# Ranking rows of a top-k gate: a row sent through DRAM, and compares cut into three parts

## The chip, the cores and the metric

The kernel runs on one core of a Trainium2 chip. The metric is the device time of one execution in microseconds (us); less is better. A core has five engines with queues of their own: TensorE (PE; its weight loads are shown as PEld), VectorE (DVE), ScalarE (ACT), GpSimd (POOL), and SyncE (SP), which here only issues DMAs. Each engine works through its instructions in the order in which they were written, and waits on semaphores for the others.

## The reference

Attention with a choice of key chunks, and then a mixture of experts in which each expert keeps at most 80 tokens. Cut to what matters here:

```python
# attention: 4 batches, 8 heads, 768 positions, head size 64  ->  x of 3072 rows of 512
logits = x @ w_gate                       # 8 experts
expert_idx = np.argmax(logits, axis=1)
probs = np.exp(logits - logits.max(-1, keepdims=True))
probs /= probs.sum(-1, keepdims=True) + 1e-09
gate_w = probs[np.arange(N), expert_idx]
for e in range(E):
    tok_idx = np.where(expert_idx == e)[0]
    if len(tok_idx) > capacity:                       # 80
        keep = np.argpartition(-gate_w[tok_idx], capacity)[:capacity]
        tok_idx = tok_idx[keep]
    h = np.maximum(x[tok_idx] @ w1[e], 0.0)
    out[tok_idx] = gate_w[tok_idx, None] * (h @ w2[e])
```

To keep the 80 strongest tokens of an expert, the kernel counts for each token how many tokens of the same expert have a larger gate value (or an equal one and an earlier place). That count is the token's rank. It is made batch by batch, 768 tokens at a time, and the batches' tables are merged.

## The kernel before, in words

The main loop has 16 rounds, `i` from 0 to 15, each for one pair of heads (4 pairs per batch). A round makes scores on TensorE (lines L512 and L527), exponentials on ScalarE (L534), masked copies and sums of exponentials on GpSimd (L548 is a select, L557 an add into `ES`), row sums on TensorE (L584 and L598) with their transpose on VectorE (L589), the transposed rows of the pair before (L644 on TensorE, scaled by L664 on VectorE and stored to DRAM by L666 through SP), the values (L571), and the preparations of later pairs: `take_q` (L442), `bounds` (L475), `bounds_out` (L482 to L494), `take_k` (L452 to L459), `unselT` (L500). The order of all instructions is written out by hand, and each engine keeps it. Loads of q, k and v are issued by SP two to four rounds ahead; one expert weight of 2 MB per round is issued by GpSimd (`wload`, L412 and L415).

A helper (`op`) keeps for each named resource who wrote and read it last, and puts in the semaphore waits. A name that two instructions write makes the second wait for the first, on the same engine too, except on TensorE.

The gate work of batch `bb` is woven into the four rounds of the next batch, `i = 4 * (bb + 1) + kk`; the last batch's comes after the loop and has functions of its own. For the first three batches:

- `kk = 0` (rounds 4, 8, 12): `gate_in`, `gate_exp`, `gate` make the gate value `gt6` (128 partitions by 6 tiles) and the chosen expert `ohb`. Near the end of the round `rank_own` (L729) multiplies each token's value with a triangle of factors that settles ties, into the scratch `T1`. Then `rank_row` spreads the 768 values of the batch along the free dimension of all partitions: six transposes on TensorE (L719) into the score bank `SC[1]`, and one copy to `G` on ScalarE (L721).
- `kk = 1` (rounds 5, 9, 13): `rank_pred` (L724) makes a copy of the row that is smaller by one part in 2^24; `rank_cmp` of tile 5 (L744) follows on VectorE, ahead of the row scaling L664. At the end of the round come `rank_diag` (L737, two instructions) and `rank_cmp` of tiles 4, 3, 2, 1, 0 (L744). Each `rank_cmp` compares 640 columns of the row, in a rotated order: from the tile behind the diagonal onwards and around, in which the smaller copy stands ahead of the true one so that one compare serves both sides of the diagonal.
- `kk = 2` (rounds 6, 10, 14): `rank_count` (L794) sums the compares per expert with 44 matmuls on TensorE, ahead of L644 of that round. `rank_slot` and, later, `rank_late` turn the counts into slots. In `kk = 3` `table` (L817) and `merge` follow.

The compares are kept in bf16 in places that hold weights only later. `Cs` gives the place, and `Ck` the resource name, which is that of the whole weight tile:

```python
def Cs(b, jt, n, lo, w):
    t, o = (w1s[E - 1], jt * S) if jt < NT - 1 else (w2s[E - 2], 2 * S)
    return bass.AP(t, o + lo, [[DB * Fd, 128], [S, n], [1, w]])
def Ck(b, jt):
    return [f"w1_{E - 1}" if jt < NT - 1 else f"w2_{E - 2}"]
```

The last batch has no rotation: `last_diag` (L756, one instruction per tile), `last_low` (L764, or two of ScalarE, L766 and L767) and `last_high` (L771) compare the columns of the diagonal, below and above it, and `last_count` (L778) uses 24 matmuls of 192 columns. Its order on the engines stands after the loop.

## Time and profile before

| | |
|---|---|
| median of 3 runs | 291.2 us (290.19 to 293.35) |
| the profiled execution | 290.18 us |
| its span, from first to last instruction | 288.4 us |
| mean granted TensorE clock | 0.997 |
| PE busy | 273.8 us (95%) |
| DVE busy | 210.4 us (73%) |
| ACT busy | 146.9 us (51%) |
| POOL busy | 227.2 us (79%) |
| DMA | 47.95 MB in 158359 packets |

Busy time counts the engine's own instructions; waiting and the issue of DMAs are not counted. In a timeline a row is: start, length, engine, line, operation, output and inputs, shapes, and how many instructions of the kind follow each other ("x5"). Behind a row, in brackets, stands idle time of the engine before it and who ended it. In a view of one line the three numbers are the shortest, the median and the longest in ns.

### The profile page before, as it was taken

What the parts mean: (1) busy time and instruction counts of PE and PEld (TensorE: products, weight loads), DVE (VectorE), ACT (ScalarE), POOL (GpSimd) and SP (SyncE); (2) the same over time, 40 slices, a digit from 0 to 9 for tenths busy, and PEclk for the clock granted to TensorE, in tenths of its full rate; (3) what the DMA queues carried; (4) which work ended last, traced back from release to release, by engine and by line L of the source; (5) the groups of instructions that cost most, each with busy time, mean ns of one, the idle gap of its engine ahead of it and who ended that gap; (6) DMA issues with size and microseconds to landing.
All of it is one profiled execution on the core that took longest, in us unless ns stands there. A gap on an engine that the chain in (4) does not pass through costs nothing.

```text
span 288.4 us, 8693 instructions
## 1 busy us (share of the span) xinstructions
PE 273.8 (95%) x3606; PEld 169.4 (59%) x3609; DVE 210.4 (73%) x575; ACT 146.9 (51%) x202; POOL 227.2 (79%) x296
## 2 busy tenths in 40 slices
PE   7995999999999999999999999999999999979991
PEld 7553465656565556656655656766565666537761
DVE  5885282739697989676979897899799888933341
ACT  2281645565657555656575556565756672603310
POOL 5059899999899999998999999989999992034532
PEclk9999999999999999999999999999999999999998
DMA  9999969989999999999999989996997959921211
GB/s 151 179 152 144 309 113 294 200 127 181 182 178 155 204 167 202 164 179 164 178 164 184 193 152 160 165 173 126 270 220 143 303 81 189 193 56 50 85 60 60
DMA packets 158359, 47.95 MB, mean 166 GB/s; under 512 B 142405, under 2 KB 150721, under 8 KB 158320
## 3 DMA queue, kind: packets, MB, share of 16 engines
q1 hardware_dynamic: 141664, 28.34, 50.0%
q0 software_dynamic: 13520, 18.67, 38.2%
q10 hardware_dynamic: 3136, 0.39, 0.9%
q8 instruction: 28, 0.46, 0.7%
q14 instruction: 11, 0.09, 0.1%
HBM read 53.49 MB, written 11.01 MB: 224 GB/s over the span
## 4 chain that ended last, share of the span: by engine, by line
PE 66%; POOL 18%; DVE 7%; DMA 4%; issue 2%; ACT 1%; ACTq 1%; POOLq 0%; DVEq 0%
PE SC L512 20%; PE OB L571 19%; POOL ES L557 12%; PE SC L527 4%; PE OB L1139 4%; PE M L598 3%; POOL EXB L548 3%; PE OB L644 3%; PE SC L1115 3%; PE M L475 3%; PE M L584 2%; PE MB L500 2%; DMA x_rows<-xp 1%; DMA qn<-in_q_dram 1%; DMA qn<-x_rows,idx 1%
## 5 line engine op out<-in xcount | busy, mean ns | idle before, releaser
L534 ACT ACTIVATE EXB<-SC 128x1024 f32<-128x1024 f32 x96 | 86.2, 917 | 46.4 <-PE SC L527 45.1
L557 POOL TENSOR_TENSOR ES<-ES,EXB 128x256 f32<-128x256 f32 (+1 forms) x105 | 101.8, 982 | 4.8
L512 PE MATMUL SC<-qT,kT 64*128 64x512 f32 (+3 forms) x512 | 96.3, 466 | 0.1
L571 PE MATMUL OB<-EXB,vn 128*64 128x256 f32 (+3 forms) x704 | 73.0, 361 | 2.9 <-POOL EXB L548 2.8
L571 PEld LDWEIGHTS OB<-EXB,vn 128*64 128x64 f32 x704 | 46.8, 137 | 26.4 <-issue 9.1
L512 PEld LDWEIGHTS SC<-qT,kT 64*128 64x128 f32 x512 | 41.4, 186 | 23.0 <-issue 14.3
L557 POOL TENSOR_TENSOR ES<-EXB 128x768 f32<-128x768 f32 (+1 forms) x30 | 46.9, 1562 | 2.5
L527 PE MATMUL SC<-unsT,ind 64*128 64x128 bf16 (+5 forms) x256 | 37.7, 289 | 0.1
L579 ACT ACTIVATE oT<-OB 128x512 f32<-128x512 f32 (+1 forms) x32 | 15.6, 489 | 42.1 <-PE OB L571 42.1
L548 POOL TENSOR_SCALAR_AFFINE_SELECT EXB<-EXB 128x256 f32<-128x256 f32 x79 | 34.1, 443 | 0.0
L589 DVE STREAM_TRANSPOSE M<-M 128x192 f32<-128x192 f32 x16 | 6.3, 394 | 23.6 <-PE M L598 23.0
L527 PEld LDWEIGHTS SC<-unsT,ind 64*128 64x128 bf16 x256 | 12.8, 95 | 17.9 <-issue 8.0
L442 DVE STREAM_TRANSPOSE qT<-qn 128x768 f32<-128x768 f32 x16 | 15.6, 975 | 7.4 <-PE SC L527 6.6
L664 DVE TENSOR_TENSOR xp<-OB,rden 128x768 bf16<-128x768 f32 x16 | 15.3, 954 | 6.6 <-PE OB L644 6.2
L446 ACT ACTIVATE rq<-qT 128x768 f32<-128x768 f32 x16 | 13.5, 843 | 8.5 <-DVE qT L442 7.9
L1092 POOL DMA_INDIRECT qn<-x_rows,idx x4 | 3.9, 987 | 17.5 <-DVE kT L1155 16.5
L452 DVE STREAM_TRANSPOSE kT<-kn 128x768 f32<-128x768 f32 x16 | 15.5, 967 | 1.3 <-DMA kn<-in_k_dram 1.3
L1145 POOL DMA_INDIRECT out_dram<-EXB,idR x6 | 5.9, 991 | 12.3 <-DVE EXB L1143 8.9
L456 DVE TENSOR_REDUCE kmm<-kT 128x24 f32<-128x768 f32 x16 | 15.2, 950 | 0.5
L457 DVE TENSOR_REDUCE kmx<-kT 128x24 f32<-128x768 f32 x16 | 15.1, 942 | 0.0
L489 DVE MAX8 top<-M 128x8 f32<-128x8 f32 (+4 forms) x160 | 14.6, 164 | 0.6
L644 PE MATMUL OB<-ident_f,oT 128*128 128x128 f32 x96 | 13.9, 281 | 0.5 <-ACT oT L579 0.5
(223 smaller groups left out, 411.5 us busy)
## 6 DMA issues: line engine op xcount, KB each, us to landing
w1s<-in_moe_w_dram POOLq DMA_DIRECT2D x8, 1024.0 KB, 9.9
w2s<-in_moe_w_dram POOLq DMA_DIRECT2D x7, 1024.0 KB, 10.7
vn<-in_v_dram SPq DMA_DIRECT2D x32, 192.0 KB, 4.5
kn<-in_k_dram SPq DMA_DIRECT2D x62, 96.0 KB, 2.7
qn<-in_q_dram SPq DMA_DIRECT2D x62, 96.0 KB, 3.1
out_dram<-w1s SPq DMA_DIRECT2D x3, 1536.0 KB, 9.1
x_rows<-xp SPq DMA_DIRECT2D x16, 192.0 KB, 5.2
out_dram<-G SPq DMA_DIRECT2D x1, 1536.0 KB, 8.2
```

Source lines behind the costliest of these rows:

```text
L442: op("dve", lambda: ve.transpose(qT[j][:], qn[s][:].rearrange("p a b c -> p (a b c)")), r=[f"qn{s}{g}" for g in range(4)], w=[f"qT{j}"])
L452: op("dve", lambda: ve.transpose(kT[j][:], kn[s][:].rearrange("p a b c -> p (a b c)")), r=[f"kn{s}{g}" for g in range(4)], w=[f"kT{j}"])
L456: op("dve", lambda: ve.tensor_reduce(kmm[j][:, 0, 0:NCH], kv, AX, ALU.min), r=[f"kT{j}"], w=[f"kmm{j}"])
L512: op("pe", lambda: pe.matmul(o, kT[j][pr, ts(kt)], qT[j][pr, q0:q1], start=True, stop=False), r=[f"kT{j}", f"qT{j}"], w=[f"SC{s}"], inc=False)
L527: op("pe", lambda: pe.matmul(o, ind[pr, ts(kt)], unsT[j][pr, b0 - 128:q1 - 128], start=False, stop=True), r=[f"ind{h}", f"unsT{j}"], w=[f" ...
L534: op("act", lambda: ac.activation(Ex(st, None, 0, W), src, ACTF.Exp, scale=SCALE), r=[f"SC{s}"], w=[f"E{st}"])
L548: op("gp", lambda: gp.affine_select(ad, a, pattern=[[0, 2], [1, 128]], compare_op=ALU.is_ge, fill=0.0, base=0, channel_multiplier=-1), r=[ ...
L557: op("gp", lambda: gp.tensor_tensor(o, in0, in1, ALU.add), r=[f"E{s2}", f"E{first[0]}"] if first else [f"E{s2}"] + kt, w=kt)
L571: op("pe", lambda: pe.matmul(OB[pr, q0:q1], vn[s][:, kt, h, :], ex, start=(n == 0), stop=last), r=[f"vn{s}{h}", "ES0" if st is None else f ...
L579: op("act", lambda: ac.activation(oT[:, q0:q1], OB[:, q0:q1], ACTF.Copy), r=[f"O{bk}"], w=[f"oT{bk}"])
L644: op("pe", lambda: pe.transpose(OB[:, ts(t)], oT[:, ts(t)], ident_f[:]), r=["oT0", "oT1", "ident_f"], w=[f"O{t // 4}"], inc=(t in (3, NT - ...
L664: op("dve", lambda: ve.tensor_tensor(xo, xi, rx, ALU.mult), r=["O0", "O1", "rden"], w=[f"xp{i % 2}"])
```

## The change

For the first three batches the gate row no longer goes through TensorE. VectorE transposes `gt6` (now 32 columns wide) in blocks of 32, SP writes the result to a DRAM tensor `gate_row` in the order of the tokens, and reads it back to all 128 partitions. `row_out` stands behind `gate` in rounds 4, 8, 12, that is behind the row store L666 on SP's queue; `row_in` stands ahead of the q and k loads of that round. Both DMAs wait in SP's queue, the second for the landing of the first.

`rank_pred` and `rank_own` are gone. The compares of all batches are those of the last batch: `diag`, `low`, `high`, in unrotated places. In the first three batches `low` of tile 5 stands where `rank_cmp` of tile 5 stood, and all others follow at the end of rounds 5, 9, 13. `count` has 24 matmuls for every batch. The resource names of the scratch places remain (`Cw`). The last batch keeps its order and its engines.

```diff
-                gt6 = al(pers, "gt6", [128, NT])
+                gt6 = al(pers, "gt6", [128, 32])
+                gtT = al(pers, "gtT", [128, 32])
...
-                def rank_row(b):
-                    for t in range(NT):
-                        gb = bass.AP(gt6, t, [[NT, 128], [0, 128]])
-                        op("pe", lambda: pe.transpose(SC[1][:, ts(t)], gb, ident_f[:]),
-                           r=["gt6", "ident_f"], w=["SC1"], inc=(t == NT - 1))
-                    op("act", lambda: ac.activation(G[:, S:2 * S], SC[1][:, 0:S], ACTF.Copy), r=["SC1"], w=["grow"])
...
+                def row_out():
+                    op("dve", lambda: ve.transpose(gtT[:], gt6[:]), r=["gt6"], w=["gtT"])
+                    o = bass.AP(gd.tensor, gd.offset, [[32, 4], [128, 32], [1, 32]])
+                    op("sp", lambda: sp.dma_start(o, gtT[:]), r=["gtT"], w=["gd"], dsem="d_gd")
+
+                def row_in():
+                    a = bass.AP(gd.tensor, gd.offset, [[0, 128], [1, S]])
+                    op("sp", lambda: sp.dma_start(G[:, S:2 * S], a), r=["gd"], w=["grow", "growA", "growB"], dsem="d_gr")
...
+                def Cw(b, jt):
+                    return Ck(b, jt) if b < B - 1 else []
...
-                def last_diag(*jts):
+                def diag(b, *jts):
                     for jt in jts:
-                        op("dve", lambda: ve.scalar_tensor_tensor(Cl(jt, jt * 128, 128), triQ[:], gt6[:, jt:jt + 1],
+                        op("dve", lambda: ve.scalar_tensor_tensor(Cl(b, jt, jt * 128, 128), triQ[:], gt6[:, jt:jt + 1],
                                                                   G[:, S + jt * 128:S + (jt + 1) * 128], ALU.mult, ALU.is_ge),
-                           r=["triQ", "gt6"] + gk(jt * 128, jt * 128 + 128), w=[f"D{jt}"])
+                           r=["triQ", "gt6"] + gk(jt * 128, jt * 128 + 128), w=[f"D{jt}"] + Cw(b, jt))
...
-                               r=["ohb", f"D{jt}"] + ([f"L{jt}"] if jt else []) + ([f"U{jt}"] if jt < NT - 1 else []),
+                               r=["ohb", f"D{jt}"] + ([f"L{jt}"] if jt else []) + ([f"U{jt}"] if jt < NT - 1 else []) + Cw(b, jt),
...
                     if live and kk == 1:
-                        rank_pred()
-                        rank_cmp(bb, 5)
+                        low(bb, 5)
...
                     if live and kk == 2:
-                        rank_count(bb)
+                        count(bb, (5, 0, 4, 1, 3, 2))
                         rank_slot(bb)
...
                         gate(bb)
+                        row_out()
...
+                    if live and kk == 0:
+                        row_in()
                     if i + 4 < NP:
                         load(i + 4, "qk")
...
-                    if live and kk == 0:
-                        rank_own(bb)
                     if live and kk == 1:
-                        rank_diag(bb)
-                        rank_cmp(bb, 4, 3, 2, 1, 0)
+                        diag(bb, *range(NT))
+                        for jt in (0, 4, 1, 3, 2):
+                            if jt:
+                                low(bb, jt)
+                            high(bb, jt)
...
-                    if live and kk == 0:
-                        rank_row(bb)
```

`low` and `high` get their scratch names in the same way as `diag`.

## The prediction

> **What bounds the kernel now.** I read the page first, for the engine that works longest and for the chain that ended last, and then the windows of four successive rounds of the loop over head pairs (a round runs from one end of L598 to the next). Times without another label are microseconds on the clock of the profile of before; "round i" is the loop index.

> ```profile
> PE 273.8 (95%) x3606; PEld 169.4 (59%) x3609; DVE 210.4 (73%) x575; ACT 146.9 (51%) x202; POOL 227.2 (79%) x296
> ...
> PE 66%; POOL 18%; DVE 7%; DMA 4%; issue 2%; ACT 1%; ACTq 1%; POOLq 0%; DVEq 0%
> ```

> TensorE sets the end, and POOL takes it over for a sixth of the chain.

> ```profile
> 59.99:73.91 13.92, 13.92 (x167) 8.36 (x165) 9.47 (x26) 7.89 (x10) 12.83 (x17) 1.00 1.02 166
> 73.91:88.49 14.58, 14.58 (x172) 8.95 (x171) 12.60 (x32) 8.70 (x13) 13.67 (x17) 1.00 1.01 174
> 88.49:104.36 15.87, 15.81 (x177) 9.22 (x179) 14.68 (x31) 8.95 (x12) 15.11 (x20) 1.00 1.18 180
> 104.36:117.23 12.87, 12.87 (x201) 7.90 (x197) 11.12 (x34) 7.54 (x10) 12.47 (x15) 1.00 1.04 187
> ```

> The columns are length, then busy time of PE, PEld, DVE, ACT and POOL. A round without gate work (3) takes 13.92 and PE fills it; POOL is 12.8 busy, so it has about one microsecond to spare. Rounds 4, 5, 6 carry gate row, compares and count of batch 0. Round 4 is longer by the 0.66 of the six transposes L719. In round 5 VectorE has 14.7 of work: its queue is where the change falls. The timeline of VectorE there, and then of POOL:

> ```profile
> 99.03 0.81 DVE L737 TENSOR_TENSOR w2s<-w2s,G 128x128 bf16<-128x128 f32 x1
> 99.87 1.30 DVE L737 TENSOR_TENSOR w1s<-w2s,G 128x640 bf16<-128x640 f32 x1
> 101.21 3.30 DVE L744 TENSOR_SCALAR w1s<-G,gt 128x640 bf16<-128x640 f32 x5
> 104.43 0.38 DVE L589 STREAM_TRANSPOSE M<-M 128x192 f32<-128x192 f32 x1
> ```

> ```profile
> 100.57 1.19 POOL L557 TENSOR_TENSOR ES<-ES,EXB 128x256 f32<-128x256 f32 x1
> 101.72 0.49 POOL L459 TENSOR_TENSOR kmm<-kmx,kmm 128x24 f32<-128x24 f32 x1
> ...
> 103.01 0.54 POOL L548 TENSOR_SCALAR_AFFINE_SELECT ES<-EXB 128x256 f32<-128x256 f32 x1
> 103.51 0.65 POOL L548 TENSOR_SCALAR_AFFINE_SELECT EXB<-EXB 128x256 f32<-128x256 f32 x1
> 104.25 1.94 POOL L557 TENSOR_TENSOR ES<-EXB 128x768 f32<-128x768 f32 x1
> ```

> The two engines take turns. The compare of 128 columns takes 0.81, though 128 elements need little: it ends 0.15 after POOL's add (98.42 to 99.69). POOL's next add but one takes 1.19 instead of its usual 0.73, since it starts only when the compare of 640 columns ends at 101.17. The same from the view of one line:

> ```profile
> L744 DVE TENSOR_SCALAR w1s<-G,gt x15: 553/570/904, 101.2 to 219.8; 128x640 bf16<-128x640 f32 x15
> L744 DVE TENSOR_SCALAR w2s<-G,gt x3: 2041/2044/2054, 89.6 to 205.5; 128x640 bf16<-128x640 f32 x3
> ```

> The same compare takes 0.55 when POOL leaves it alone and 2.04 when it starts just behind POOL's 1.81 add. So each compare issued during an add waits that add out, and POOL then goes first again before the next compare. Last, TensorE at the place where the compares are used:

> ```profile
> 104.76 0.28 PE L527 MATMUL SC<-unsT,ind 64*128 64x256 bf16 x2
> 104.96 0.28 PE L794 MATMUL MB<-w2s,ohb 128*32 128x32 bf16 x8
> 105.07 0.60 PE L794 MATMUL MB<-w1s,ohb 128*32 128x64 bf16 x36
> 105.60 0.88 PE L644 MATMUL OB<-ident_f,oT 128*128 128x128 f32 x6
> ```

> The count L794 starts as soon as the scores end. The last compare ended at 104.51, 0.4 before: there is almost no slack between VectorE's compares and TensorE.

> **The change, part by part.** *Gate row.* Six transposes (L719) and their copy (L721, 0.81 on ACT) go. They are on TensorE's path: -0.66 per batch. L724 (0.83, ACT) goes too and is worth nothing, for ACT is 51% busy. L729 (1.40, VectorE, end of round 4) goes, worth nothing: VectorE idles 1.26 after it. Added is one transpose of 128x32 on VectorE; by L589 (0.40 for 192 columns) and the smallest rows (0.16) it costs 0.2, hidden because VectorE's bound scores are ready about 0.8 before TensorE asks for them in round 4.

> *Two DMAs on SP.* In round 4 SP is behind: it issues the row store L666 at 83.94, though its data were ready at 78.07. So the write of the gate row issues near 84.5, and SP, which now waits for its landing, issues the read that much later. The row store of that round landed 3.45 after its issue; so the read goes out near 87.9, and POOL's weight load, issued at 87.34 or 0.7 earlier, runs against it. The nearest rows for the read bound it by 2.0 (an idle-queue load of kn) and 10.0 (kn issued at 88.07). I take 3.5, because it has 128 pieces of 3 KB where a load has 768 of 128 bytes, but shares with the weights: landed near 91.4. Its first reader, the compare of tile 5, would then wait about 2.4 on VectorE; the row scaling L664 behind it ends 1.0 late and so does everything on VectorE up to the chain of compares. In rounds 8 and 12 SP is not behind that far (L666 at 136.65 and 194.15) and the read lands before its reader. Queued behind the wait on SP are the q, k and v loads; they have two rounds to land and keep some 7 of slack, so nothing there.

> *Compares.* Seven instructions in the end of round 5 (two L737, five L744) become fifteen: six diagonal ones of 128 columns, and nine low or high parts of 128 to 640. From the last batch's rows, a diagonal is 0.346 and a part 0.281 (128 columns) to 0.554 (640), that is about 0.21 fixed and the rest by columns. The scratch tile is one resource in the bookkeeping, so each compare waits for the one before and they follow 0.04 apart. Undisturbed this is 6 x 0.39 + 9 x 0.25 + 1.67 = 6.2, to 105.3. Now the turns with POOL, in order from 99.03. D0, D1, D2 each wait out one of the adds that end at 99.69, 100.49, 101.29: done 101.42. D3 to D5 run while POOL issues its weight load: 102.57. High 0 shares with the first select, 103.24; low 4, 103.78. POOL's 768-column add takes the port until 105.46: high 4, 105.53. Low 1 beside a select: 105.89. The 1.27 add: high 1, 107.44. Low 3 beside a select: 107.92. The 1.28 add: high 3, 109.21. Then POOL has no more exponentials to add, and low 2 and high 2 end at 110.04. The same bookkeeping gives 104.49 for the chain of before, where the trace has 104.51. Bounds: 105.3 (no turns) to 110.5 (if the chain starts 1.0 late, as in batch 0).

> *Count.* 24 matmuls replace 44 over as many columns, so 0.64 stays. From the second tile on, each waits for the last compare, because all name the same scratch tile: 20 of the 24 come after 110.08 and take 0.53. Behind them on TensorE stand L644 and the last scores. L644 starts at 110.6 instead of 105.60: +5.0 per batch. VectorE's L589 also waits, but its scaled rows are due only at 113.0, before the values want them (113.7).

> [...]

> *Clock.* TensorE would idle from 105.0 to 110.1, 5.1 long. The trace shows an idle gap of 2.77 (22.6 to 25.38) after which the matmuls ran as before, and the end, where the last matmul ends at 282.59 and the clock reads half from 286.9, 4.3 later:

> ```profile
> 282.60:286.80 4.20, 0.00 (x0) 0.00 (x0) 0.48 (x1) 0.00 (x0) 0.97 (x1) 1.00 0.21 81
> 286.90:288.40 1.50, 0.00 (x0) 0.00 (x0) 0.00 (x0) 0.00 (x0) 0.00 (x0) 0.50 0.00 0
> ```

> At the start L884's matmuls came 0.107 apart from 1.75 to 7.0 and 0.056 after: 5.25 at half speed cost 2.6. So per gap 0 to 2.6. 5.1 lies nearer to the gap that fell, but with 0.8 to spare on one sample; I take half, 1.3 per batch. [...]

> *Sum.* 3 x (-0.66 + 5.0) = 13.0; batch 0's late row 0.4; clock 3.9: +17.3. The profiled execution took 290.18 (span 288.4, 1.8 around it); the median of the runs shown is 291.2. 290.18 + 17.3 = 307.5, and half a microsecond towards the median: 308.

> **The rivals.** *The row lands behind the weights.* If the read is held like kn at 88.07, it lands near 98, the compare of tile 5 and L664 wait, and TensorE loses 6 more in batch 0: 314; in all three batches 326. For it: three of four kn loads there took 9.4 or more. Against: its pieces are few, and in batches 1 and 2 it is issued earlier.
> *The turns cost little.* Then the chain ends at 105.3, L644 starts at 105.9, +0.3 - 0.66 per batch: 289.1, or 290 at the median. Against: every compare of round 5 that met an add waited for it.
> *Faster.* The compares end before TensorE asks (104.9), so the transposes' 0.66 is won and also the 0.27 by which POOL's held-up adds delay L598 in round 5: 3 x 0.93 = -2.8, 287.4 to 288.2. What decides is the chain's end: the three waits for long adds would have to vanish and the fixed cost to fall by a few hundredths each. I see nothing for that but the shorter work per instruction.

> **How the numbers follow.** Forecast 0.78, row behind weights 0.09, little cost 0.07, faster 0.06. From the forecast's bounds: without any loss of clock 303.6, with all of it 311.5; one add less in each chain takes 3.8 off (300), a late row adds 6 to a case without clock loss or 2 to the top. So 300.5 to 314. About 1% is what a measurement can tell here; faster by more 0.05, within 0.08, slower 0.87.

> **What would show it.** Right: fifteen compares in rounds 5, 9, 13, several over 1.2; L589 of rounds 6, 10, 14 about 5.5 later in its round; a gap of some 5 in PE ahead of the second tile of the count; no L719. Wrong: compares of 0.3 to 0.6 throughout, or a gap of PE ahead of L571 in round 5 (the row). A clock below 1 after the gaps tells how much of the term was due.

## The result, and the profile after

The changed kernel takes 311.06 us (309.89 to 311.52, 4 runs) against 291.5 (290.19 to 293.35, 4 runs) before: 1.066 times, interval 1.059 to 1.073. The profiled execution took 311.52, its span 309.6 against 288.4. Of some kernels below the executions differ by several per cent from one to the next; their ratio leaves out those more than 1.5% above the fastest, so the whole spread stands beside it.

The page of the changed kernel: the engines, the granted clock in 40 slices, the chain that ended last, and the count's group, whose last column is TensorE's idle time ahead of it.

```profile
PE 279.8 (90%) x3528; PEld 173.2 (56%) x3531; DVE 215.8 (70%) x600; ACT 142.4 (46%) x196; POOL 221.8 (72%) x296
...
PEclk9997999999999979999999689999998699999997
...
PE 64%; DVE 23%; DMA 5%; issue 3%; POOL 3%; ACTq 1%; POOLq 0%; DVEq 0%
...
L760 PE MATMUL MB<-w1s,ohb 128*32 128x192 bf16 x60 | 2.6, 324 | 13.5 <-DVE w1s L753 13.5
```

TensorE waits 13.5 us for the high compares (L753), in three places. VectorE, 7% of the chain before, is now 23%, and the clock has dips where it had none.

The windows of rounds 4, 5 and 6 (length, then busy time of PE, PEld, DVE, ACT and POOL, then the clock, the DMA share and GB/s):

```profile
75.52:89.44 13.92, 13.92 (x166) 8.36 (x165) 11.36 (x32) 7.91 (x11) 12.94 (x17) 1.00 0.96 163
89.44:110.91 21.47, 16.54 (x185) 10.13 (x185) 17.44 (x39) 9.97 (x12) 19.26 (x24) 1.00 1.05 173
110.91:124.90 13.99, 13.79 (x167) 8.50 (x167) 10.80 (x34) 5.85 (x8) 7.44 (x10) 0.88 1.00 179
```

Round 4 has lost its 0.66 of transposes. The stretch of round 5 is 5.6 longer than before, and TensorE works only 16.5 of its 21.5. The next is over 1 us longer at a clock of 0.88. The end of round 5 on VectorE:

```profile
101.19 2.24 DVE L738 SCALAR_TENSOR_TENSOR w1s<-triQ,gt,G 128x128 bf16<-128x128 f32 x5
...
105.41 2.06 DVE L753 TENSOR_SCALAR w1s<-G,gt 128x512 bf16<-128x512 f32 x1
107.51 0.44 DVE L746 TENSOR_SCALAR w1s<-G,gt 128x384 bf16<-128x384 f32 x1
107.99 1.25 DVE L753 TENSOR_SCALAR w1s<-G,gt 128x256 bf16<-128x256 f32 x1
...
109.68 1.38 DVE L753 TENSOR_SCALAR w1s<-G,gt 128x384 bf16<-128x384 f32 x1
```

and on POOL:

```profile
105.38 1.81 POOL L558 TENSOR_TENSOR ES<-EXB 128x768 f32<-128x768 f32 x1
...
107.82 1.26 POOL L558 TENSOR_TENSOR ES<-ES,EXB 128x512 f32<-128x512 f32 x1
...
109.58 1.26 POOL L558 TENSOR_TENSOR ES<-EXB 128x512 f32<-128x512 f32 x1
```

Each of the three long adds catches one compare, which ends 0.2 to 0.3 behind it: 2.06, 1.25 and 1.38 for work of 0.48, 0.35 and 0.41. The short compare between two adds runs at 0.44. TensorE meanwhile:

```profile
106.44 0.27 PE L760 MATMUL MB<-w2s,ohb 128*32 128x192 bf16 x4
111.11 0.60 PE L760 MATMUL MB<-w1s,ohb 128*32 128x192 bf16 x20 [4.41 <-DVE w1s L753]
```

Four matmuls of the count, then 4.41 idle until the last compare of the chain has ended. And these are windows inside the three stretches at half clock, the clock in the last column but two. The first stretch begins 0.7 behind its gap, the others 1.1 and 0.6 before theirs end:

```profile
111.80:115.15 3.35, 3.35 (x16) 2.24 (x17) 1.79 (x5) 0.00 (x0) 0.00 (x0) 0.50 0.89 146
173.30:180.00 6.70, 5.65 (x52) 3.87 (x60) 3.52 (x9) 0.68 (x1) 0.39 (x1) 0.50 0.83 159
238.10:244.85 6.75, 6.18 (x68) 4.30 (x76) 4.79 (x17) 1.22 (x3) 1.69 (x3) 0.50 0.64 160
```

Two intervals read from the traces sort all that follows. In the changed kernel's lines, A runs from the transpose of the row sums, L590, at the start of round 5 (9, 13) to the first row transpose L645 in round 6 (10, 14): it holds the compares and the wait for them. B runs from there to L590 at the end of that round; it holds no waits for compares, only TensorE's own work at whatever clock it has.

| kernel | median (spread), us | span | A, three batches | B, three batches |
|---|---|---|---|---|
| before | 291.5 (290.19 to 293.35) | 288.4 | 17.04, 17.08, 17.07 | 11.70, 11.69, 12.93 |
| after | 311.06 (309.89 to 311.52) | 309.6 | 22.13, 22.25, 21.47 | 13.32, 13.88, 15.39 |
| e1_row_only | 294.41 (290.71 to 302.82) | 289.0 | 17.37, 17.37, 17.58 | 11.70, 11.69, 13.95 |
| e2_cmp_only | 314.58 (313.98 to 315.18) | 313.3 | 22.25, 22.25, 22.71 | 14.15, 14.02, 14.61 |
| e3_no_adds | 299.9 | 298.2 | 18.29, 23.83, 19.34 | 11.70, 11.70, 14.09 |
| e3b_before_no_adds | 290.49 | 288.7 | 17.04, 17.04, 17.05 | 11.69, 11.69, 12.93 |
| e4_names | 305.18 (301.3 to 307.47) | 303.2 | 21.03, 21.11, 16.75 | 13.26, 13.20, 15.03 |
| e5_warm | 309.65 (301.54 to 311.44) | 309.2 | 30.33, 21.86, 21.31 | 11.70, 11.69, 12.93 |
| e6_diag2 | 307.9 (306.5 to 309.3) | 304.1 | 20.68, 22.03, 22.30 | 11.69, 13.35, 14.71 |
| e10_cmp_no_adds | 299.17 | 297.4 | 18.56, 18.56, 19.26 | 11.70, 11.70, 14.21 |
| e12_cmp_warm | 304.9 (303.47 to 305.36) | 301.7 | 21.88, 21.88, 20.85 | 11.70, 11.70, 12.93 |

The span grew by 21.2: A by 14.7, B by 6.3; rounds 4, 8 and 12 give back 2.0; a half clock at the start costs 1.6; what follows the row sums of the last round takes 0.9 more, and round 15 takes 0.3 less.

### The profile page after: what moved, and what is told of

The parts are those of the page before. It is cut to its first block, busy times and chain, and to the rows that moved or that the text cites. A ratio compares the mean times of both kernels' runs of the same rounds, so it can differ in the third digit from the quotient of the medians.

```text
span 309.6 us, 8562 instructions
## 1 busy us (share of the span) xinstructions
PE 279.8 (90%) x3528; PEld 173.2 (56%) x3531; DVE 215.8 (70%) x600; ACT 142.4 (46%) x196; POOL 221.8 (72%) x296
## 4 chain that ended last, share of the span: by engine, by line
PE 64%; DVE 23%; DMA 5%; issue 3%; POOL 3%; ACTq 1%; POOLq 0%; DVEq 0%
PE SC L513 20%; PE OB L572 18%; PE OB L645 4%; PE SC L528 4%; DVE w1s L746 4%; PE OB L1108 3%; DVE w1s L753 3%; PE SC L1084 3%; DVE w1s L738 3%; PE M L599 2%; PE M L476 2%; DVE kmm L457 2%; DMA G<-gate_row 2%; DVE qT L443 2%; PE M L585 2%
## 5 line engine op out<-in xcount | busy, mean ns | idle before, releaser
L558 POOL TENSOR_TENSOR ES<-ES,EXB 128x256 f32<-128x256 f32 (+1 forms) x105 | 100.3, 968 | 4.8
L513 PE MATMUL SC<-qT,kT 64*128 64x512 f32 (+3 forms) x512 | 99.8, 481 | 0.1
L572 PE MATMUL OB<-EXB,vn 128*64 128x256 f32 (+3 forms) x704 | 74.7, 367 | 2.9 <-POOL EXB L549 2.8
L572 PEld LDWEIGHTS OB<-EXB,vn 128*64 128x64 f32 x704 | 48.0, 140 | 27.6 <-issue 11.0
L513 PEld LDWEIGHTS SC<-qT,kT 64*128 64x128 f32 x512 | 43.5, 195 | 23.2 <-issue 17.2
L549 POOL TENSOR_SCALAR_AFFINE_SELECT EXB<-EXB 128x256 f32<-128x256 f32 x79 | 33.2, 432 | 18.3 <-ACT EXB L535 18.3
L528 PE MATMUL SC<-unsT,ind 64*128 64x128 bf16 (+5 forms) x256 | 38.7, 297 | 0.1
L590 DVE STREAM_TRANSPOSE M<-M 128x192 f32<-128x192 f32 x16 | 6.3, 395 | 27.2 <-PE M L599 26.9
L447 ACT ACTIVATE rq<-qT 128x768 f32<-128x768 f32 x16 | 13.5, 844 | 10.1 <-DVE qT L443 9.8
L645 PE MATMUL OB<-ident_f,oT 128*128 128x128 f32 x96 | 15.9, 308 | 0.5 <-ACT oT L580 0.5
L760 PE MATMUL MB<-w1s,ohb 128*32 128x192 bf16 x60 | 2.6, 324 | 13.5 <-DVE w1s L753 13.5
```

The lines of the kernel that those rows point to most:

```text
L513: op("pe", lambda: pe.matmul(o, kT[j][pr, ts(kt)], qT[j][pr, q0:q1], start=True, stop=False), r=[f"kT{j}", f"qT{j}"], w=[f"SC{s}"], inc=False)
L528: op("pe", lambda: pe.matmul(o, ind[pr, ts(kt)], unsT[j][pr, b0 - 128:q1 - 128], start=False, stop=True), r=[f"ind{h}", f"unsT{j}"], w=[f" ...
L549: op("gp", lambda: gp.affine_select(ad, a, pattern=[[0, 2], [1, 128]], compare_op=ALU.is_ge, fill=0.0, base=0, channel_multiplier=-1), r=[ ...
L558: op("gp", lambda: gp.tensor_tensor(o, in0, in1, ALU.add), r=[f"E{s2}", f"E{first[0]}"] if first else [f"E{s2}"] + kt, w=kt)
L572: op("pe", lambda: pe.matmul(OB[pr, q0:q1], vn[s][:, kt, h, :], ex, start=(n == 0), stop=last), r=[f"vn{s}{h}", "ES0" if st is None else f ...
L645: op("pe", lambda: pe.transpose(OB[:, ts(t)], oT[:, ts(t)], ident_f[:]), r=["oT0", "oT1", "ident_f"], w=[f"O{t // 4}"], inc=(t in (3, NT - ...
```

## The experiments

Two theories stood against each other at first: "turns" (each compare that meets an add waits for its end, so the cutting into fifteen costs the time) and "row" (the DRAM turn costs it). Later "many instructions" (fifteen are too many even undisturbed) and the clock were set apart.

### One part alone: the row, or the compares

e1_row_only has the DRAM row with the seven rotated compares and 44 matmuls of before:

```diff
                     if live and kk == 1:
-                        rank_pred()
                         rank_cmp(bb, 5)
                     scores(i, 2, 4)
+                    if live and kk == 1:
+                        rank_pred()
...
                         gate(bb)
+                        row_out()
...
+                    if live and kk == 0:
+                        row_in()
                     if i + 4 < NP:
                         load(i + 4, "qk")
...
-                        rank_row(bb)
```

> The row of the first three batches through DRAM as in the change, the rotated compares and the 44-matmul count as before; the smaller copy of the row (L724's work) moved behind the scores of stages 2 and 3 so that ScalarE does not stand in front of a late row. Theory 'turns' (compares and GpSimd adds take turns at one port, and the count waits for the last compare): the row itself is harmless, -0.66 per batch, and in batch 0 about +1.7 because the row lands late (a gap of 0.7 ahead of the values, compares 1 us later): about 290 us in the profile, 288.5 to 291.5. Rival 'row' (the round trip on SP is what costs): 296 or more. Rival 'many instructions' (fixed cost of each compare): like 'turns' here.

Its profiled execution took 290.71, ratio 1.0047 with an interval of 0.999 to 1.010: A grows by 0.3 to 0.5 and B of the third batch by 1.0, which eats the 2.0 of the transposes. But 5 of its 12 executions lie between 297 and 303; the last part of this section comes back to them.

e2_cmp_only is the other half: the changed kernel with TensorE's row.

```diff
                         gate(bb)
-                        row_out()
...
-                        row_in()
...
+                    if live and kk == 0:
+                        rank_row(bb)
```

> The compares and the count of the change, the row made by TensorE and ScalarE as before. 'Turns': the whole loss, plus the transposes' 0.66 per batch, less 0.4 for the late row of batch 0: 311 to 314 us. Rival 'row': 291 to 293 us.

314.58, ratio 1.081 (1.075 to 1.087): the compares alone cost more than the whole change. The row through DRAM is not what made the changed kernel slow.

### Why the compares take so long

```diff
-    for (s2, c2, q0, q1) in ADDS[st] if i < NP - 1 else []:
+    for (s2, c2, q0, q1) in ADDS[st] if i < NP - 1 and not (i % 4 == 2 and i > 4 and st in (1, 2, 3)) else []:
```

This edit takes POOL's adds of stages 1 to 3 out of rounds 6, 10 and 14, so the sums of those rounds lack these exponentials. It was made in the changed kernel and, as a control, in the kernel before. These two and e10 below were executed once each.

> The changed kernel, with GpSimd's adds of stages 1, 2 and 3 left out in rounds 6, 10, 14 (those exponentials are then missing from the sums): nothing to take turns with while the fifteen compares run on. 'Turns': no compare over 0.9 us after the first three, the chain ends about 3.5 us earlier, TensorE's gap ahead of the count falls from 4.4 to 4.9 down to about 1.5, and the clock stays full in those rounds: 293 us (291 to 295). 'Many instructions': chain and gap stay, 309 to 312 us.

> The control for e3_no_adds: the kernel before without the same adds. 'Turns' and 'many instructions' both: 289 to 290.5 us, at most 1 us less than before, since GpSimd sets the end for only 0.3 us in the rounds of the compares.

The control is unmoved (290.49, A 17.04). The changed kernel came to 299.9, between both theories, but in the second batch its row landed 7.56 us after its issue and TensorE stood 4.9 for it: A is 23.83 there, 18.29 and 19.34 in the others. So it was done again without the DRAM row, the same edit in e2:

> The e2_cmp_only kernel (TensorE's row, the new compares and count) without GpSimd's adds of the exponentials of stages 1 to 3 in rounds 6, 10 and 14, so the sums of those rounds lack these exponentials; no row through DRAM, so no late row as in e3_no_adds. Theory 'turns' (each compare that meets an add waits for that add's end): the chain of 15 compares takes its own lengths, and what is left is e3's first batch, 1.25 us over before: 290.5 (before without these adds) + 3 x 1.25 = 294, range 291.5 to 297. Theory 'many instructions': 306 to 312, little below e2's 314.6.

299.17, above the range of "turns" and far below "many instructions". The high compares of the changed kernel and of e10 (count, then minimum, median and maximum in ns), each line from the view of its source line:

```profile
L753 DVE TENSOR_SCALAR w1s<-G,gt x15: 305/517/2062, 103.6 to 238.2; 128x640 bf16<-128x640 f32 x3, 128x128 bf16<-128x128 f32 x3, 128x512 bf16<-128x512 f32 x3, 128x256 bf16<-128x256 f32 x3
```

```profile
L760 DVE TENSOR_SCALAR w1s<-G,gt x15: 301/485/579, 103.9 to 226.9; 128x640 bf16<-128x640 f32 x3, 128x128 bf16<-128x128 f32 x3, 128x512 bf16<-128x512 f32 x3, 128x256 bf16<-128x256 f32 x3
```

Without the adds no high compare is over 0.58 (of the low ones behind the diagonal, one took 0.91). From e2 to e10 A falls by 3.7, 3.7 and 3.5 and B by 2.5, 2.3 and 0.4, together 16.0 of e2's 24.9 over before. What is left in A, 1.5, 1.5 and 2.2, is the price of fifteen pieces with the adds of round 5 still there (the first three diagonal compares take 0.70 to 0.80 each, against 0.35 for the others). I had taken 1.25 for it from one batch, and nothing for the clock and the end: against the control, B of the third batch lost 1.3 and the part after the last row sums 2.1; 1.5 of that is one idle stretch of TensorE ahead of L572, for which the profile names no releaser.

e4_names takes the name of the whole scratch tile from the compares, so that none waits for the one before, and the count waits for parts:

```diff
-    r=["triQ", "gt6"] + gk(...), w=[f"D{jt}"] + Cw(b, jt))
+    r=["triQ", "gt6"] + gk(...), w=[f"D{jt}"])
```

(and so for L and U).

> The changed kernel, in which the compares no longer write the name of the whole scratch tile: a compare does not wait for the one before, and a matmul of the count waits for the three parts of its own tile only. 'Turns': the adds still pin the chain; by the same bookkeeping it ends 0.9 earlier, and 16 of the last 20 matmuls of the count slip into the gap, so L645 comes about 1.4 earlier per batch: 306.5 us (304 to 309), with the clock as it was. Rival 'one name' (the serial waits are the cause): most of the loss gone, 292 to 297 us.

305.18, ratio 1.042 (1.033 to 1.052), as expected: A falls by only 1.1 in two batches. The third batch was not expected, and it is the plainest witness of all. The same fifteen compares, and the chain is over 4 us shorter; VectorE in the third batch:

```profile
229.88 0.48 DVE L753 TENSOR_SCALAR w1s<-G,gt 128x512 bf16<-128x512 f32 x1
...
231.12 0.41 DVE L753 TENSOR_SCALAR w1s<-G,gt 128x384 bf16<-128x384 f32 x1
```

and POOL there:

```profile
229.65 2.18 POOL L413 DMA_DIRECT2D w1s<-in_moe_w_dram  x1 [1.64 <-DMA out_dram<-w1s]
...
232.70 1.81 POOL L558 TENSOR_TENSOR ES<-EXB 128x768 f32<-128x768 f32 x1
```

Here POOL's weight load had to wait 1.64 for a store that reads the same buffer, and took 2.18 to issue, against 0.79 in the second batch. The 768-column add therefore began at 232.70, after the last compare (231.53), and none of them met it. In the first two batches of the same execution the compares from the 512-column one on met all three and took 2.04, 1.36 and 1.49. A is 16.75 there, below that of before. In the third batch of the changed kernel the same load waited 1.54, but took only 0.79 to issue, and two of the three adds were met.

The first batch of e5_warm (further below) shows it with the names as they were and with no add left out. A late row pushed its chain so far back that no add of POOL fell among the compares:

```profile
106.71 1.89 DVE L738 SCALAR_TENSOR_TENSOR w1s<-triQ,gt,G 128x128 bf16<-128x128 f32 x5
...
112.29 0.42 DVE L753 TENSOR_SCALAR w1s<-G,gt 128x384 bf16<-128x384 f32 x1
```

```profile
113.41 1.81 POOL L558 TENSOR_TENSOR ES<-EXB 128x768 f32<-128x768 f32 x1
```

From the first start to the last end the fifteen take 6.0 there, and 9.9, 10.7 and 9.9 in the three batches of the changed kernel; the seven of before take 5.4 to 5.5.

e6_diag2 does the diagonal in two instructions, as before, with the product L729 put back: eleven compares instead of fifteen.

```diff
-                        diag(bb, *range(NT))
+                        diag2(bb)
...
+                    if live and kk == 0:
+                        rank_own(bb)
```

> The changed kernel with the diagonal parts made in two instructions as before (with the product at the end of rounds 4, 8, 12): 11 instructions instead of 15. 'Turns' (one long add fewer to wait for): the chain ends about 1.9 earlier, the gap is near 2.7, and where the gap is short enough the clock holds: 305 us if the clock is lost as often as before, 300 if not. 'Many instructions': 6 diagonals of 0.39 against 0.25 and 0.80, 1.1 less per batch, 308 us.

The time, 307.9 (ratio 1.058, 1.051 to 1.065), is the number of the rival, but not by its mechanism. In the second and third batch the chain ends 21.0 and 21.3 after the row sums of round 5, with fifteen pieces 21.3 and 20.5: four instructions fewer, and the last long add still pins the end. Only in the first, where a late row (5.40 from issue to landing) pushed the whole chain back, did the diagonal miss the adds of round 5, and there no later compare met one either; A is 20.68 with the wait for the row inside.

### What the half clock costs

e5_warm puts 18 matmuls of 512 columns into the gap, on a bank that nothing reads:

```diff
-                        count(bb, (5, 0, 4, 1, 3, 2))
+                        count(bb, (5, 0, 4, 1, 3, 2), (18, 0, 0, 0, 0, 0))
```

> The changed kernel with 18 idle-filling matmuls of 512 columns (3.9 us at full clock) behind the first tile of the count in rounds 6, 10, 14, so that TensorE is busy during most of its wait. If the half clock behind the gaps costs what the trace says (1.6 + 2.2 + 2.5): granted clock 1.0 in these rounds, and 6 us less, 305 us (303.5 to 306.5). If the clock after the gaps costs nothing: 311 us.

B is 11.70, 11.69 and 12.93, to 0.01 that of before. The median is 309.65 all the same. In the profiled execution (310.96) the row of the first batch landed 9.4 after its issue; the other executions were not traced. The view of the read's line in e5, who waited for it and how long it took:

```profile
  DVE w2s L746: 9.0, 1
...
DMA to landing us min/median/max: 3.4/3.7/9.4
```

The fastest execution took 301.54. The same fillers in e2, where no row can be late:

> The e2_cmp_only kernel with 18 matmuls of 512 columns into a free bank behind the first tile's count, in the 5 us in which TensorE waits for the second; nothing is taken out and no row goes through DRAM. Theory 'the half clock costs 6 us in all': from the row transposes of rounds 6, 10 and 14 to the next row sums, 14.15, 14.02 and 14.61 us in e2 against 11.70, 11.69 and 12.93 in before, so 314.6 - 6.5 = 308, range 306 to 310. Theory 'the half clock is hidden behind VectorE and ScalarE': 313 to 315.

304.9, 9.7 less than e2. Between the two profiled executions, whose spans are 11.6 apart, B fell by 6.5 as worked out, from 14.15, 14.02 and 14.61 to the values of before; the third chain met fewer adds (A less by 1.9), the first two gain 0.7, and the part after the last row sums is 2.4 shorter: 1.5 of that is an idle stretch of TensorE ahead of L572 in e2, for which the profile names no releaser, and its cause stays open. The clock row of the page, of e2 and then of e12:

```profile
PEclk9997999999999959999999789999998799999999
```

```profile
PEclk9997999999999999999999999999999999999997
```

### The row that is sometimes late

e9_row_late5 moves e1's first compare behind the row scaling.

```diff
-                        rank_cmp(bb, 5)
                     scores(i, 2, 4)
...
                         scale_rows(i - 1)
+                        if live and kk == 1:
+                            rank_cmp(bb, 5)
```

> As e1_row_only, and the compare of tile 5 stands behind the row scaling on VectorE, so that a late row holds up nothing that TensorE needs. 'Turns': the gap ahead of the values in batch 0 goes, 0.7 to 1.5 us less than e1_row_only: 288.5 to 289.5 us, that is about 0.5% faster than before. If the late row was no cost: equal to e1_row_only.

298.97, from 289.59 to 301.44, where 288.5 to 289.5 had been expected. Its profiled execution was one of the long ones (296.53), and TensorE's waits name the cause:

```profile
PE OB L575 <- DMA vn<-in_v_dram: 2.7, 1, 2.7
```

That v load was issued at 103.55, 0.09 after a weight load of POOL, and landed 9.52 later. With the wait and the half clock behind it B of the first batch is 16.45 instead of 11.70; the mean granted clock of this execution is 0.984, against 0.997 in before's. SP, having stood over the landing of the row's store (2.0 to 2.7 from the store's issue to the read's), now issues its loads that much later, and some fall behind a weight load. The row itself goes the same way. Over the profiles with the DRAM row, by how long before the read the weight load had been issued:

| weight load issued before the read by, us | read lands after, us |
|---|---|
| issued 1.2 to 4.7 after the read, 18 cases | 3.3 to 4.0 |
| issued 0.3 after it (e11, the read itself behind eight loads) | 5.0 |
| 0.05, 0.19 (e6, e3) | 3.6, 3.7 |
| 0.71, 0.74, 0.73 (e9, after, e6) | 4.7, 5.1, 5.4 |
| 1.5, 2.1, 2.3 (e11, e5, e3) | 12.1, 9.4, 7.6 |

Two ways out were tried on e9. In e11_row_behind the read is issued behind the eight loads of q and k, so that SP never stands still:

```diff
-                    if live and kk == 0:
-                        row_in()
                     if i + 4 < NP:
                         load(i + 4, "qk")
+                    if live and kk == 0:
+                        row_in()
```

> The e9_row_late5 kernel (row through DRAM, compares of before, that of tile 5 behind the row scaling), but the read back of the row is issued behind the eight loads of q and k instead of ahead of them, so that SyncE no longer stands idle over the store's landing (2.0 to 2.7 us a batch in e1 and e9) with eight loads behind it. Theory 'SyncE's queue': the runs of e1 and e9 at 295 to 303 us are those in which the loads behind the row slid into the landing of a weight load (e9's profile: a vn load issued at 103.55 landed 9.52 later, and TensorE waited 2.7 for it). Without the wait the loads go as before; the row itself is asked for last and may land 5 to 10 us late, which the first compare, behind the row scaling, still covers: all runs between 288 and 291.5, median 289.5. Rival 'something else in the compares or the adds': the spread stays, median 296 to 300. Rival 'the row is late': the first compare of round 6 waits, 292 to 296.

302.33 (300.1 to 304.33), worse than e9. I had overlooked the readers. Who waited for the row, and its landing times:

```profile
  ACT G L730: 10.4, 2
  DVE w2s L750: 9.0, 1
```

The row landed 12.1 after its issue in the first batch, VectorE held nine microseconds at the compare, ACT stood at its copy of the row with the exponentials behind it, and TensorE idled 7.9. In e13_weights_later every weight load goes behind the first two score stages of the next round:

```diff
-                    if 0 < i < NP - 2:
-                        wload((i - 1) // 2, (i - 1) % 2)
...
+                    if 1 < i < NP - 1:
+                        wload((i - 2) // 2, (i - 2) % 2)
                     scores(i, 2, 4)
```

> The e9_row_late5 kernel with every weight load moved from the end of its round to behind the first pair of score stages of the next, some 2 to 5 us later on GpSimd; SyncE's order is that of e9. Theory 'weights' (a transfer issued after a weight load lands with it, 5 to 11 us later, one issued 1 us ahead of it lands in 3.3 to 3.7): the row and the loads behind it are through before the weight load starts, so all runs lie between 288 and 292, median 290. If SyncE's wait alone decides, whatever the weights do: as e9, 296 to 300. If the later weight load only meets the next round's loads instead: 294 to 300 with a wait for qn, kn or vn elsewhere.

300.58 (298.61 to 302.35), so not the version hoped for either. The row landed in 4.0, 3.7 and 3.9, as the theory says, and the clock row of the page reads 9 in every slice but the last, which reads 7. The store of the row now ran behind the weight load instead: from its issue to the read's SP took 9.0 and 5.8 in the first and third batch, without a trace in A, which is 18.2 in all three. But POOL issues the load in the middle of its stage now, and rounds 2 and 3, which hold no gate work, take 14.45 and 14.43 instead of 13.92, round 4 14.93. The long executions of e1 were not traced; that they are like e9's is an inference. No version here is faster than the kernel before.

## Why the prediction was right, by its steps

- **Transposes**: -0.66 a batch forecast; rounds 4, 8 and 12 fell from 14.58, 14.57 and 13.78 to 13.92, 13.92 and 13.12.
- **Turns, and the wait of the count**: +5.0 a batch forecast, +5.1, +5.2 and +4.4 measured. The chain was worked out to end 21.5 after the row sums of round 5; it ended at 21.6, 21.3 and 20.5. Each long add met a compare that stands two places later than forecast in the first batch and one place later in the second, with little effect on the end; in the third batch only two were met. Undisturbed, the fifteen were put at 6.2; the first batch of e5 took 6.0. e10 gives the shares: 3.5 to 3.7 of A's growth goes with the long adds, the rest with the pieces themselves and the adds of round 5. The one port of which the prediction and the theory speak is the author's picture: no run shows it, only that in the changed kernel each compare that met a long add ended 0.1 to 0.3 behind it.
- **Row**: the read was to take 3.5 and land at 91.4; it took 5.05 and landed at 94.0, and L746 waited 3.3 instead of 2.4. Of the 2.6 between the two times 1.0 is that the changed kernel came to round 5 later, at the row sums. TensorE lost 0.7 ahead of L572 in round 5, where the prediction had looked for a sign of the row, though the profile names no releaser for it; A is no longer in that batch than in the next. In the second and third batch it landed in 3.5 and 3.3.
- **Clock**: mis-sized. 3.9 was forecast, taking half of 2.6 per gap, the author's estimate from the two gaps of before's trace; B shows 1.6, 2.2 and 2.5, together 6.3, and e12 shows that it is the clock. All three gaps, of 4.41, 4.92 and 4.15, tripped it, and two of the half-speed stretches lasted 6.8.
- **Not in the sum**: in round 0 TensorE has the same 2.77 gap in all fourteen profiles of this study, before's among them, and in nine of them the clock then ran at half, in before's not, in after's yes, for 1.6. It may be part of the scatter of both kernels, of which one execution each was traced. Of the 0.9 after the last row sums 0.7 is an idle stretch of TensorE ahead of L843, for which the profile names no releaser; its cause stays open.

So 17.3 was forecast against before's profile and 21.2 came. Of the 3.9 between them 2.4 is the clock, 1.6 the start and 0.9 the end; the stall came 0.3 short of its 15.0, the late row showed none of its 0.4, and round 15 gave 0.3.

The rival "the row lands behind the weights" did not decide here: the four executions of the changed kernel lie within 1.6 of each other. But it is real: e3, e5 and e11 show it with waits of TensorE of 4.9, 6.7 and 7.9. The prediction had priced it at 6. "Faster" would have needed the chain to miss the long adds; the third batch of e4 did so, and there the count was not late.

## What to carry to other kernels

Where VectorE and POOL take turns, the cost of cutting an instruction lies less in its fixed time (1.5 to 2.2 a batch here) than in the foreign instructions that the longer chain then meets (3.5 to 3.7); look at what POOL does in the microseconds into which the chain is stretched. A stall of TensorE had a second price behind it here, the half clock (1.6 to 2.5 a gap in the changed kernel), that can be read by itself from the same work after the gap. And the round trip on SP's queue was two costs: the wait that holds back every load queued behind it (2.0 to 2.7 in e1 and e9), and a landing time that jumped to between 7.6 and 12.1 where a weight load of 1 MB had been issued 1.5 to 2.3 ahead of the read, from between 3.3 and 4.0 where the load came 1.2 or more behind it.
